# Cross-covariance attention and a multiplicative feed-forward: the start of batch one in another order

## The chip, the cores and the metric

The kernel runs on one core of one Trainium2 chip. The metric is the device time of one execution in microseconds (us). A core has five engines that run side by side: TensorE (PE, matmuls; PEld are its weight loads), VectorE (DVE), ScalarE (ACT), GpSimd (POOL) and SyncE (SP). Each works through its own list of instructions in order; an instruction waits for semaphores, and whatever stands behind it on its engine waits too. Transfers are issued by SP, ACT or POOL and carried out by DMA engines. A transfer that changes the type (here fp32 in memory to bf16 on chip) is issued by POOL in this kernel, plain stores and transposing transfers by SP.

## The reference

Four batches of 5824 rows with 256 columns pass through attention over the columns, then all 23,296 rows through the feed-forward:

```
qn = q / (norm of q's columns + 1e-6);  kn likewise
s  = kn^T @ qn / tau                      # 256 x 256 per batch
a  = softmax(s, last axis)
x  = v @ a                                # 5824 x 256 per batch
out = ((x @ w1) * (x @ w2)) @ w3 @ w_out  # 256 -> 1024 -> 1024 -> 256
```

tau is 1. All matrices come in fp32 and the output is fp32.

## The kernel before

**Two foldings of weights.** The kernel never computes x. It multiplies each batch's softmax matrix into w1 and w2 once (`fold`, `narrow`; the result is `Wf`), so that the products a = v @ (A w1) and b = v @ (A w2) come straight from v. Once for all batches it computes W = w3 @ w_out (`W_sb`, 1024 x 256), in eight units (`w_unit`), each of eight matmuls of 256 columns (L878). Each unit needs a part of w3 turned by a transposing transfer (`w3T_0` to `w3T_3`, two units each).

**Pieces and slots.** A batch of q, k or v is laid out with 45 rows to a partition and one short rest of 64 rows. It is loaded in six pieces: five of 8 rows per partition, and the last of 5 plus the rest (`LAST` is 5, the rest lies in the place behind). Loads round to bf16 on the way. Of v a piece must be turned, columns to partitions (`vT`): by TensorE in halves of four rows (`transpose_half_on_pe`, eight matmuls and a copy by VectorE) or by a transposing transfer of SP (`transpose_piece`).

The main loop goes over chunks of 512 rows (index `c`, two chunks to a piece) and, within a chunk, over eight blocks of 128 of the 1024 hidden columns (index `j`). One turn is a slot (`emit_ab`): two matmuls of 512 columns for `a`, two for `b`, a copy of `a` to bf16 by ScalarE (`as`, L662) and a multiply by VectorE (`abh`, L673). `a` and `b` use four PSUM banks in turn ("ab"); the folds, transpositions and W units mostly use three others ("out"). A slot's output matmuls come later (`pend`), in batch one only from slot 32 on, once W is there. From chunk 4 on a product scheme with seven instead of eight block products is used.

**The start of batch one.** There is nothing to compute on until q and k of batch one are on chip. TensorE follows their loads: `squares` (L259) accumulates q^T q, of which the diagonal gives the norms, and `products` (L271) accumulates q^T k into `G`. The squares of k are shared: for most of k ScalarE squares the rows and VectorE adds them up in `kacc` (L246, L247), for the end TensorE does it as for q. `busy` and `busy_long` are matmuls on constants that keep TensorE running while it waits for loads.

The functions of `soft_units(0)` then make the softmax matrix. Before the change: `k_early` folds `kacc` to 256 columns with a copy and an add (L282, L283), `k_first` takes the diagonal of k's squares and adds it (L287, L289), `k_row` sums over the partitions with a matmul against ones (L340, 256 columns in fp32) and turns the sum into 1/(root + 1e-6) in four ScalarE steps over 256 columns (L348: Ln, Exp with 0.5, Ln with 1e-6 added, Exp with -1). `q_first` reduces q's diagonal (L357), `scaled_first` multiplies `G` by k's factors (L379), makes q's factors and takes the exponentials (L384). `first_folds` and `second_quarter` make the first 512 columns of `Wf` in narrow steps, `soft0[8]` to `soft0[11]` the other 512 (L427).

The later batches have all the time of the batch before them and do the norms in another way: a reduce on VectorE which transposes blocks of 32 (L301), a small matmul against `fold4` (L309), the same four steps over 16 columns (L315), and a transposing copy that spreads the factors over the row (L322).

**What sets the order.** The order of instructions is that of the program's text. Within a batch an agenda (`at(t, cost, fn)`) holds steps with a due time against `clock`, which counts the time of TensorE's work as the program adds it up; at each slot `run_due` emits what is due. So a due time moves an instruction in every engine's list that it touches. POOL's list holds the loads, and between them small copies (`gate`, `hold`) whose only purpose is to make POOL wait: for a product of a slot, or for a transposing transfer. Eight loads of POOL are tracked at a time, so a load also waits for the landing of the eighth before it. SP's list holds the transposing transfers and the stores.

Before the change POOL issues, at the end of the start: q's last piece (its rest, then rows 0; 1 and 2; 3; 4), the first half of v's piece 0, w1 and w2 in column blocks 0 to 255, 256 to 511 and 512 to 1023, the second half of v's piece 0, v's pieces 1 and 2, w_out, w3. Slots run chunk by chunk, so chunk 0 needs all columns of w1 and w2 first, and chunk 1, from the second half of v's piece 0, comes at slot 8.

Of the kernel before, what the change touches and what calls it, by code (L numbers as in the profile page):

```python
# [10 lines left out]
ALU = mybir.AluOpType  # L11
# [3 lines left out]
P = 128  # L15
# [10 lines left out]
def kernel(  # L26
# [250 lines left out]
    def soft_units(n):  # L277
        st = {}

        def k_early():  # L280
            st["kk"] = work.tile([P, C], F32, tag="kk", name="kk", bufs=1)
            nc.vector.tensor_copy(st["kk"], kacc[0][:, 0, :])  # L282
            nc.vector.tensor_add(st["kk"], kacc[0][:, 1, :], st["kk"])  # L283

        def k_first():
            d = work.tile([P, CT, P], F32, tag="sq", name="dk", bufs=2)
            nc.vector.tensor_mul(d, S["k"], ident.unsqueeze(1).to_broadcast([P, CT, P]))  # L287
            d = st["ksq"] = d.rearrange("p c t -> p (c t)")
            nc.vector.tensor_add(d, d, st["kk"])  # L289

        def scaled_first():
            for ct in range(CT):
# [2 lines left out]
            exps(0)  # L295
            exps(1)

        def norms():

            red = work.tile([P, 16], F32, tag="red", name=f"red_{n}", bufs=1)  # L300
            nc.vector.tensor_reduce(  # L301
                out=red, in_=accs[n].rearrange("p w (b j) -> p (w b) j", j=32),
                axis=mybir.AxisListType.X, op=ALU.add, apply_transpose=True,
            )
            st["red"] = red

        def totals():
# [3 lines left out]
            )  # L311

        def norm_step(i):
            t = st["tot"][:, :16]
            nc.scalar.activation(  # L315
                out=t, in_=t, func=(AF.Ln, AF.Exp)[i % 2],
                scale=(1.0, 0.5, 1.0, -1.0)[i], bias=eps_t if i == 2 else 0.0,
            )

        def spread():  # L320
            st["kr"] = work.tile([P, C], F32, tag="kr", name=f"kr_{n}", bufs=1)
            nc.vector.transpose(  # L322
                st["kr"].rearrange("p (b j) -> p b j", j=32),
                st["tot"][:, 8:16].unsqueeze(2).to_broadcast([P, 8, 32]),
            )

        def pick():
# [9 lines left out]
        def k_row():  # L337

            m = psum.tile([P, 512], F32, name=f"row_{n}", **bank("ab"))
            nc.tensor.matmul(m[:, :C], lhsT=ones_pp, rhs=st["ksq"], start=True, stop=True)  # L340
            st["row"] = m[:, :C]
            st["kr"] = work.tile([P, C], F32, tag="kr", name=f"kr_{n}", bufs=1)
            for i in range(4):
                k_step(i)

        def k_step(i):
            kr = st["kr"]
            nc.scalar.activation(  # L348
                out=kr, in_=kr if i else st["row"], func=(AF.Ln, AF.Exp)[i % 2],
                scale=(1.0, 0.5, 1.0, -1.0)[i], bias=eps_t if i == 2 else 0.0,  # L350
            )

        def diagonal(src):
            d = work.tile([P, CT, P], F32, tag="sq", name=f"dq_{n}", bufs=2)
# [147 lines left out]
    def at(t, cost, fn):  # L502
        seq[0] += 1
        agenda.append((t, seq[0], cost, fn))
# [13 lines left out]
        return vTt[:, ct, :]  # L518

    last_ab = [None]  # L520
    halves = [None, None]
    slot = [0]
    due_sums = []
    following = []
# [125 lines left out]
    def emit_ab(b, c, j):  # L650
        n = chunk_cols(c)
        tiles = []
        for w in range(2):
            t = psum.tile([P, 512], F32, name=f"{'ab'[w]}_{b}_{c}_{j}", **bank("ab"))
            for ct in range(CT):
                nc.tensor.matmul(  # L656
                    t[:, :n], lhsT=Wf[b][:, ct, w, j * P : (j + 1) * P], rhs=rhs_of(b, c, ct),
                    start=(ct == 0), stop=(ct == CT - 1),
                )
            tiles.append(t)  # L660
        a_sb = work.tile([P, 512], BF16, tag="a_sb", name=f"as_{b}_{c}_{j}", bufs=4)
        nc.scalar.copy(a_sb[:, :n], tiles[0][:, :n])  # L662
        if c == NCH - 1:
            if b % 2 == 0 and j == 0:
                lefts[b // 2] = work.tile([P, FT, 2, P + LEFT], BF16, tag="left", name=f"left_{b}", bufs=1)
            both = lefts[b // 2][:, j, b % 2, :]
            nc.vector.tensor_mul(both, a_sb[:, :n], tiles[1][:, :n])
            ab = both[:, :P] if b % 2 == 0 else both[:, LEFT:]
        else:
            if j % 4 == 0:  # L670
                halves[j // 4] = in_pool.tile([P, 4, 512], BF16, tag="big", name=f"abh_{b}_{c}_{j}", bufs=BIG_BUFS)
            ab = halves[j // 4][:, j % 4, :]
            nc.vector.tensor_mul(ab, a_sb, tiles[1])  # L673
        last_ab[0] = ab
        slot[0] += 1
        if not seven(b, c):
            if b == B - 1 or c == NCH - 1:
                lag = LAG if b == B - 1 else FT + LAG_FAST
                pend.append((slot[0] + lag, 1, lambda only=None: emit_out(b, c, j, ab, only)))
            elif j == FT - 1:  # L680
                for i in range(FT):
                    fn = lambda i=i, ab2=tuple(halves): emit_half(b, c, i, ab2)
                    pend.append((slot[0] + 1 + LAG_FAST + i, 1, fn))
        elif j == FT - 1:
            sums, groups = seven_products(b, c, *halves)
            for i, fn in enumerate(sums):
                due_sums.append((slot[0] + 2 * i, fn))
            ready = slot[0] + 1 + (LAG_FAST if b < B - 1 else 0)
            for i, group in enumerate(groups):
                wait = 0 if b == B - 1 else i  # L690
                pend.append((ready + wait, 2, lambda group=group: [fn() for fn in group]))
        clock[0] += 4 * (n * MM_COL + MM_FIX)
# [94 lines left out]
    wout_sb = w3_wout[:, FT * F : FT * (F + D)].rearrange("p (l d) -> p l d", d=D)  # L787
    w3T = []

    def transpose_w3():  # L790

        for h in range(FT // 2):
            m = in_pool.tile([P, 2, FT, P], BF16, tag="big", name=f"w3T_{h}", bufs=BIG_BUFS)
            nc.sync.dma_start_transpose(m, w3_bf[:, 2 * h : 2 * h + 2, :])
            w3T.append(m)
# [39 lines left out]
    for pi in range(1, 4):  # L835
# [2 lines left out]
        products(pi, whole)  # L838
        if pi < 3:
            busy_long(pi)  # L840
    load_piece("q", 0, 5, (1, 3, 4))
    new_piece("v", 0, 0)
    load_part("v", 0, 0, 0, half)
    for f0, f1 in ((0, 256), (256, 512), (512, F)):
        nc.gpsimd.dma_start(out=w12[:, :, 0, f0:f1], in_=w1r[:, :, f0:f1])
        nc.gpsimd.dma_start(out=w12[:, :, 1, f0:f1], in_=w2r[:, :, f0:f1])
    load_part("v", 0, 0, half, PIECE)
    load_piece("v", 0, 1)
    load_piece("v", 0, 2)
    nc.gpsimd.dma_start(out=wout_sb, in_=moe_w_out.rearrange("(lh ll) c -> ll lh c", ll=P))  # L850
# [9 lines left out]
        squares("q", 4, sl)  # L860
        products(4, sl)
    soft0[1]()
    for sl in ([LAST, 0], [1, 2], [3]):
        squares("q", 5, sl)
        products(5, sl)
    squares("q", 5, [4], end=True)
    soft0[2]()
    products(5, [4], end=True)
    soft0[3]()
    soft0[6]()  # L870
    busy(2)
# [35 lines left out]
    def make_agenda(b):  # L907
# [3 lines left out]
        if b == 0:  # L911
            at(0.5, 0.87, soft0[5])
            for i in range(4):
                at((1.7, 2.6, 3.5, 3.9)[i], 0.43, soft0[8 + i])
            at(4.6, 0.5, lambda: transpose_half_on_pe(0, 0, 1, False))
            at(7.0, 0.5, lambda: transpose_half_on_pe(0, 1, 0, False))
            at(8.0, 0.5, lambda: transpose_half_on_pe(0, 1, 1, False))
            at(15.0, 0.0, transpose_w3)
            at(15.0, 0.0, lambda: transpose_piece(0, 2))
            for jt in range(FT):  # L920
                at(28.3 + 1.2 * jt, 0.87, lambda jt=jt: w_unit(jt))
            moves = [("qk", 1, 0, 29.0), ("qk", 1, 1, 29.2), ("v", 0, 3, 33), ("qk", 1, 2, 49), ("qk", 1, 3, 56)]
            moves += [("qk", 1, 4, 62), ("v", 0, 4, 68), ("qk", 1, 5, 79), ("v", 0, 5, 88)]
            moves += [("v", 1, 0, 99), ("v", 1, 1, 110), ("qk", 2, 0, 122)]
# [5 lines left out]

        for nm, m, pi, t in moves:
            if nm == "qk" and m == 1 and pi in (0, 2):
                at(t, 0.0, lambda pi=pi: hold(vTs[0][0][:1, (2 + pi // 2) * PIECE, 0, :1]))
            at(t, 0.0, gate)
            if nm == "qk":
                at(t, 0.0, lambda m=m, pi=pi: load_qk(m, pi))
            else:
                at(t, 0.0, lambda m=m, pi=pi: load_piece("v", m, pi))
                at(t + (2.5 if (m, pi) == (0, 4) else 4.0), 0.0, lambda m=m, pi=pi: transpose_piece(m, pi))
# [20 lines left out]

    for b in range(B):
        make_agenda(b)
        for c in range(NCH):
            for j in range(FT):
                run_due()
                while following:
                    following.pop(0)()
                scores_due(c * FT + j)
                emit_ab(b, c, j)
                lag = 0  # L970
                if b == B - 1 and c >= NCH - 2:
                    lag = LAG_END if c == NCH - 1 else LAG + (LAG_END - LAG) * (j + 1) // FT
                room = 2
                while slot[0] > W_SLOT and len(pend) > lag and pend[0][0] <= slot[0] and pend[0][1] <= room:
                    _, size, fn = pend.pop(0)
                    fn()
                    room -= size
                    run_due()
                while due_sums and due_sums[0][0] <= slot[0]:
                    due_sums.pop(0)[1]()  # L980
        run_due(1e9)

    n = len(pend)
# [37 lines left out]
```

## Time and profile before

| | |
|---|---|
| median of three executions | 556.06 us (555.81 to 557.0) |
| the profiled execution | 555.26 us |
| its span, first to last instruction | 553.5 us |
| TensorE busy in the span | 541.7 us (98%) |
| VectorE, ScalarE, GpSimd busy | 435.1, 376.8, 305.4 us |
| granted TensorE clock | 1.00 throughout |
| first matmul of `a` | 36.94 us after the span's start |
| k's last load of batch one lands | 28.97 us |
| moved by DMA | 77.61 MB, mean 140 GB/s |

The page's rows read: line of the program, engine, operation, output<-input with the shapes, count, then busy us in all, mean ns of one, and the idle time of the engine in front of them with what ended it. Rows of the order of instructions read: start and duration in us, engine, line, operation, and, in brackets, idle time before it. Rows of the chain of waits read: start, length in us, what it was. TensorE's matmuls are pipelined: the duration in a row is longer than the distance to the next row, and it is the distance that counts.

### The profile page before, as it was taken

What the parts mean: (1) busy time and instruction counts of PE and PEld (TensorE: products, weight loads), DVE (VectorE), ACT (ScalarE), POOL (GpSimd) and SP (SyncE); (2) the same over time, 40 slices, a digit from 0 to 9 for tenths busy, and PEclk for the clock granted to TensorE, in tenths of its full rate; (3) what the DMA queues carried; (4) which work ended last, traced back from release to release, by engine and by line L of the source; (5) the groups of instructions that cost most, each with busy time, mean ns of one, the idle gap of its engine ahead of it and who ended that gap; (6) DMA issues with size and microseconds to landing.
All of it is one profiled execution on the core that took longest, in us unless ns stands there. A gap on an engine that the chain in (4) does not pass through costs nothing.

```text
span 553.5 us, 12324 instructions
## 1 busy us (share of the span) xinstructions
PE 541.7 (98%) x4623; PEld 353.0 (64%) x4630; DVE 435.1 (79%) x787; ACT 376.8 (68%) x757; POOL 305.4 (55%) x259
## 2 busy tenths in 40 slices
PE   7799999999999999999999999999999999999997
PEld 4565577666666666666667566666666666666665
DVE  5558747899976787988876788888877688988984
ACT  5446647788866777777766777777766666566663
POOL 4260021778788678889887488898987400010000
PEclk9999999999999999999999999999999999999999
DMA  9999989985666878576554777775550245443102
GB/s 215 210 177 209 175 159 206 215 203 96 160 124 155 189 153 163 127 145 138 129 126 120 153 156 157 165 142 125 146 115 40 84 116 116 93 110 80 77 40 97
DMA packets 75260, 77.61 MB, mean 140 GB/s; under 512 B 54208, under 2 KB 59072, under 8 KB 75200
## 3 DMA queue, kind: packets, MB, share of 16 engines
q0 software_dynamic: 15904, 38.93, 40.2%
q1 hardware_dynamic: 58928, 37.17, 24.0%
q8 instruction: 36, 0.59, 0.4%
q10 hardware_dynamic: 368, 0.72, 0.4%
q14 instruction: 24, 0.20, 0.1%
HBM read 78.91 MB, written 23.86 MB: 186 GB/s over the span
## 4 chain that ended last, share of the span: by engine, by line
PE 93%; DMA 5%; DVE 0%; ACT 0%; issue 0%; POOL 0%; POOLq 0%
PE a L656 28%; PE b L656 28%; PE prodA L569 13%; PE prodC L569 6%; PE G L200 5%; PE prodB L569 3%; DMA k<-in_k_dram 3%; PE o L704 3%; PE fold L427 2%; DMA q<-in_q_dram 2%; PE o_out L735 2%; PE w L878 1%; PE G L271 0%; PE narrow L451 0%; POOL k L120 0%
## 5 line engine op out<-in xcount | busy, mean ns | idle before, releaser
L673 DVE TENSOR_TENSOR abh<-as,b 128x512 bf16<-128x512 bf16 x352 | 240.2, 684 | 82.8 <-ACT as L662 77.8
L662 ACT CAST as<-a 128x512 bf16<-128x512 f32 (+1 forms) x384 | 215.4, 562 | 93.7 <-PE a L656 61.4
L656 PE MATMUL a<-vT,Wf 128*128 128x512 bf16 x704 | 209.4, 379 | 0.1
L656 PE MATMUL b<-vT,Wf 128*128 128x512 bf16 x704 | 209.4, 379 | 0.0
L656 PEld LDWEIGHTS <-Wf 128*128 128x128 bf16 x1536 | 141.1, 98 | 100.6 <-issue 0.5
L569 PEld LDWEIGHTS <-S 128*128 128x128 bf16 x1248 | 82.6, 98 | 34.3 <-issue 0.2
L212 DVE TENSOR_TENSOR acc<-acc,sq 128x512 f32<-128x512 f32 x132 | 91.6, 694 | 3.0 <-ACT sq L197 1.9
L579 ACT COPY osb<-prodA 128x256 f32<-128x256 f32 x156 | 58.1, 372 | 42.0 <-PE prodA L569 41.4
L588 POOL TENSOR_TENSOR S<-abh,abh 128x1024 bf16<-128x1024 bf16 x29 | 61.7, 2126 | 31.7 <-DVE abh L673 16.6
L569 PEld LDWEIGHTS <-abh 128*128 128x128 bf16 x936 | 62.0, 98 | 25.7 <-issue 0.2
L591 POOL TENSOR_TENSOR S<-S,abh 128x1024 bf16<-128x1024 bf16 x29 | 61.7, 2127 | 1.9
L591 POOL TENSOR_TENSOR S<-abh,S 128x1024 bf16<-128x1024 bf16 x29 | 61.8, 2132 | 0.1
L591 POOL TENSOR_TENSOR S<-abh 128x1024 bf16<-128x1024 bf16 x29 | 61.8, 2130 | 0.1
L644 POOL COPY gate_t<-abh 1x1 bf16<-1x1 bf16 x39 | 7.2, 185 | 79.9 <-DVE abh L673 79.7
L569 PE MATMUL prodA<-comb_T,S 128*128 128x128 bf16 x624 | 47.6, 219 | 0.0
L200 PE MATMUL G<-k,q 128*128 128x256 bf16 x276 | 47.0, 273 | 0.0
L197 ACT ACTIVATE sq<-q 128x512 f32<-128x512 bf16 x69 | 43.8, 634 | 0.0
L197 ACT ACTIVATE sq<-k 128x512 f32<-128x512 bf16 x69 | 43.3, 628 | 0.0
L582 DVE TENSOR_TENSOR osb<-prodC,osb 128x256 f32<-128x256 f32 x78 | 32.6, 417 | 0.0
L648 POOL COPY gate_t<-vT 1x1 bf16<-1x1 bf16 x2 | 0.4, 176 | 53.1 <-DMA vT<-v 53.1
L200 PEld LDWEIGHTS <-q 128*128 128x128 bf16 x276 | 23.9, 98 | 3.6
L569 PE MATMUL prodB<-W_sb,abh 128*128 128x128 bf16 x312 | 23.8, 219 | 0.1
(137 smaller groups left out, 467.8 us busy)
## 6 DMA issues: line engine op xcount, KB each, us to landing
out_dram<-osb SPq DMA_DIRECT2D x44, 512.0 KB, 3.4
k<-in_k_dram POOLq DMA_DIRECT2D x19, 512.0 KB, 8.3
v<-in_v_dram POOLq DMA_DIRECT2D x19, 512.0 KB, 5.3
q<-in_q_dram POOLq DMA_DIRECT2D x18, 512.0 KB, 5.3
w_wout<-in_moe_w_dram POOLq DMA_DIRECT2D x1, 2048.0 KB, 22.4
k<-in_k_dram POOLq DMA_DIRECT2D x4, 320.0 KB, 7.0
v<-in_v_dram POOLq DMA_DIRECT2D x4, 320.0 KB, 5.4
q<-in_q_dram POOLq DMA_DIRECT2D x3, 320.0 KB, 5.0
```

Of the source, the lines that this page charges most:

```text
L197: nc.scalar.activation(out=sqs[0][:, :, part, :], in_=src[:, o : o + 2, :], func=AF.Square)
L200: nc.tensor.matmul(G[:, ct, :], lhsT=qt[:, i, ct * P : (ct + 1) * P], rhs=kt[:, i, :], start=(pr == 0 and part == 0 and ct == 0), stop=(pr ...
L212: nc.vector.tensor_add(accs[n], accs[n], sqs[0][:, part - 2])
L569: nc.tensor.matmul(st[nm][:, i, :], lhsT=a[:, j, i * P : (i + 1) * P], rhs=w[j], start=(first and j == 0 and i == 0), stop=(j == 3), skip_ ...
L579: nc.scalar.copy(quarter(r, d), st["A"])
L582: nc.vector.tensor_add(quarter(r, d), st[nm], quarter(r, d))
L588: adder.tensor_add(x, a21, a22)
L591: adder.tensor_sub(x, u, w)
L656: nc.tensor.matmul(t[:, :n], lhsT=Wf[b][:, ct, w, j * P : (j + 1) * P], rhs=rhs_of(b, c, ct), start=(ct == 0), stop=(ct == CT - 1),)
L662: nc.scalar.copy(a_sb[:, :n], tiles[0][:, :n])
L673: nc.vector.tensor_mul(ab, a_sb, tiles[1])
L704: nc.tensor.matmul(t[:, k, :], lhsT=ab2[j // 4][:, j % 4, (2 * h + k) * P : (2 * h + k + 1) * P], rhs=W_sb[:, j, :], start=(j == 0 and k = ...
```

## The change

It has six parts, all of them in batch one.

1. The norms of k are made as in the later batches: `k_early` and `k_first` reduce with transposition (to eight columns), `k_row` multiplies by `fold4`, takes the four steps over eight columns in PSUM, and spreads.
2. q's last piece comes in two transfers besides its rest (rows 0 to 2; 3 and 4) instead of four, and the last squares of q are those of rows 3 and 4 together, ahead of the products of both.
3. The second half of v's piece 0 is loaded ahead of the columns 512 to 1023 of w1 and w2, instead of after them.
4. The first 16 slots go by halves: chunk 0 with j = 0 to 3, chunk 1 with j = 0 to 3, chunk 0 with j = 4 to 7, chunk 1 with j = 4 to 7. The two tiles of a chunk's products are allotted together at j = 0. The due times of v's transpositions and of the last four folds move with this.
5. Of the transposing transfers, v's piece 2 goes ahead of the last part of w3; the two W units that need this part are due later, behind slot 32.
6. GpSimd's hold before the loads of batch 2's first q and k waits for the last part of w3 instead of v's piece 2.

```diff
         def k_early():
-            st["kk"] = work.tile([P, C], F32, tag="kk", name="kk", bufs=1)
-            nc.vector.tensor_copy(st["kk"], kacc[0][:, 0, :])
-            nc.vector.tensor_add(st["kk"], kacc[0][:, 1, :], st["kk"])
+            red = work.tile([P, 16], F32, tag="red", name="red_acc", bufs=1)
+            partition_sums(red, kacc[0].rearrange("p w (b j) -> p (w b) j", j=32))
+            st["kk"] = work.tile([P, 8], F32, tag="kk", name="kk", bufs=1)
+            nc.vector.tensor_add(st["kk"], red[:, :8], red[:, 8:])
 
         def k_first():
             d = work.tile([P, CT, P], F32, tag="sq", name="dk", bufs=2)
             nc.vector.tensor_mul(d, S["k"], ident.unsqueeze(1).to_broadcast([P, CT, P]))
-            d = st["ksq"] = d.rearrange("p c t -> p (c t)")
-            nc.vector.tensor_add(d, d, st["kk"])
+            red = work.tile([P, 16], F32, tag="red", name="red_end", bufs=1)
+            partition_sums(red[:, :8], d.rearrange("p c (b j) -> p (c b) j", j=32))
+            st["ksq"] = work.tile([P, 8], F32, tag="ksum", name="ksum", bufs=1)
+            nc.vector.tensor_add(st["ksq"], red[:, :8], st["kk"])
...
+        def partition_sums(dst, src):
+
+            nc.vector.tensor_reduce(out=dst, in_=src, axis=mybir.AxisListType.X, op=ALU.add, apply_transpose=True)
+
+        def root_step(t, i):
+
+            nc.scalar.activation(
+                out=t, in_=t, func=(AF.Ln, AF.Exp)[i % 2],
+                scale=(1.0, 0.5, 1.0, -1.0)[i], bias=eps_t if i == 2 else 0.0,
+            )
...
         def k_row():
 
             m = psum.tile([P, 512], F32, name=f"row_{n}", **bank("ab"))
-            nc.tensor.matmul(m[:, :C], lhsT=ones_pp, rhs=st["ksq"], start=True, stop=True)
-            st["row"] = m[:, :C]
-            st["kr"] = work.tile([P, C], F32, tag="kr", name=f"kr_{n}", bufs=1)
+            t = m[:, :8]
+            nc.tensor.matmul(t, lhsT=fold4.rearrange("p g j -> p (g j)"), rhs=st["ksq"], start=True, stop=True)
             for i in range(4):
-                k_step(i)
...
+                root_step(t, i)
+            spread(t)
...
-            if j % 4 == 0:
-                halves[j // 4] = in_pool.tile([P, 4, 512], BF16, tag="big", name=f"abh_{b}_{c}_{j}", bufs=BIG_BUFS)
-            ab = halves[j // 4][:, j % 4, :]
+            if j == 0:
+                halves[c] = [
+                    in_pool.tile([P, 4, 512], BF16, tag="big", name=f"abh_{b}_{c}_{h}", bufs=BIG_BUFS) for h in range(2)
+                ]
+            ab = halves[c][j // 4][:, j % 4, :]
...
-    load_piece("q", 0, 5, (1, 3, 4))
+    load_piece("q", 0, 5, (3,))
     new_piece("v", 0, 0)
     load_part("v", 0, 0, 0, half)
     for f0, f1 in ((0, 256), (256, 512), (512, F)):
         nc.gpsimd.dma_start(out=w12[:, :, 0, f0:f1], in_=w1r[:, :, f0:f1])
         nc.gpsimd.dma_start(out=w12[:, :, 1, f0:f1], in_=w2r[:, :, f0:f1])
-    load_part("v", 0, 0, half, PIECE)
+        if f0 == 256:
+            load_part("v", 0, 0, half, PIECE)
...
-    for sl in ([LAST, 0], [1, 2], [3]):
+    for sl in ([LAST, 0], [1, 2]):
         squares("q", 5, sl)
         products(5, sl)
-    squares("q", 5, [4], end=True)
+    squares("q", 5, [3, 4], end=True)
     soft0[2]()
-    products(5, [4], end=True)
+    products(5, [3, 4], end=True)
...
-                at((1.7, 2.6, 3.5, 3.9)[i], 0.43, soft0[8 + i])
-            at(4.6, 0.5, lambda: transpose_half_on_pe(0, 0, 1, False))
-            at(7.0, 0.5, lambda: transpose_half_on_pe(0, 1, 0, False))
-            at(8.0, 0.5, lambda: transpose_half_on_pe(0, 1, 1, False))
-            at(15.0, 0.0, transpose_w3)
+                at((5.3, 6.2, 7.1, 8.0)[i], 0.43, soft0[8 + i])
+            at(2.5, 0.5, lambda: transpose_half_on_pe(0, 0, 1, False))
+            at(11, 0.5, lambda: transpose_half_on_pe(0, 1, 0, False))
+            at(14, 0.5, lambda: transpose_half_on_pe(0, 1, 1, False))
+            at(15.0, 0.0, lambda: transpose_w3(range(FT // 2 - 1)))
             at(15.0, 0.0, lambda: transpose_piece(0, 2))
+            at(15.0, 0.0, lambda: transpose_w3([FT // 2 - 1]))
             for jt in range(FT):
-                at(28.3 + 1.2 * jt, 0.87, lambda jt=jt: w_unit(jt))
+                t = 28.3 + 1.2 * jt if jt < FT - 2 else 37.0 + 1.3 * (jt - FT + 2)
+                at(t, 0.87, lambda jt=jt: w_unit(jt))
...
-                at(t, 0.0, lambda pi=pi: hold(vTs[0][0][:1, (2 + pi // 2) * PIECE, 0, :1]))
+                at(t, 0.0, lambda pi=pi: hold(w3T[-1][:1, 0, 0, :1] if pi == 0 else vTs[0][0][:1, 3 * PIECE, 0, :1]))
...
-        for c in range(NCH):
-            for j in range(FT):
+        order = [(c, j) for c in range(NCH) for j in range(FT)]
+        if b == 0:
+            order[: 2 * FT] = [(c, h * 4 + j) for h in range(2) for c in range(2) for j in range(4)]
+        for s, (c, j) in enumerate(order):
```

More of the change, by code (lines that the diff above doesn't have):

```diff
@@ L296, in scaled_first @@
             exps(1)
+        def partition_sums(dst, src):
[5 more added lines that the diff above has]
+            )
         def norms():
             red = work.tile([P, 16], F32, tag="red", name=f"red_{n}", bufs=1)
[L301 to L304, printed above, removed]
+            partition_sums(red, accs[n].rearrange("p w (b j) -> p (w b) j", j=32))
             st["red"] = red
@@ L313, in norm_step, with spread @@
         def norm_step(i):
[L314 to L320, printed above, removed]
+            root_step(st["tot"][:, :16], i)
+        def spread(src=None):
+            src = st["tot"][:, 8:16] if src is None else src
             st["kr"] = work.tile([P, C], F32, tag="kr", name=f"kr_{n}", bufs=1)
@@ L323, in spread @@
                 st["kr"].rearrange("p (b j) -> p b j", j=32),
-                st["tot"][:, 8:16].unsqueeze(2).to_broadcast([P, 8, 32]),
+                src.unsqueeze(2).to_broadcast([P, 8, 32]),
             )
@@ L339, in k_row @@
             m = psum.tile([P, 512], F32, name=f"row_{n}", **bank("ab"))
-            nc.tensor.matmul(m[:, :C], lhsT=ones_pp, rhs=st["ksq"], start=True, stop=True)
-            st["row"] = m[:, :C]
-            st["kr"] = work.tile([P, C], F32, tag="kr", name=f"kr_{n}", bufs=1)
+            t = m[:, :8]
+            nc.tensor.matmul(t, lhsT=fold4.rearrange("p g j -> p (g j)"), rhs=st["ksq"], start=True, stop=True)
             for i in range(4):
-                k_step(i)
[L346 to L351, printed above, removed]
+                root_step(t, i)
+            spread(t)
         def diagonal(src):
@@ L520 @@
     last_ab = [None]
-    halves = [None, None]
+    halves = {}
     slot = [0]
@@ L681, in emit_ab @@
                 for i in range(FT):
-                    fn = lambda i=i, ab2=tuple(halves): emit_half(b, c, i, ab2)
+                    fn = lambda i=i, ab2=tuple(halves[c]): emit_half(b, c, i, ab2)
                     pend.append((slot[0] + 1 + LAG_FAST + i, 1, fn))
         elif j == FT - 1:
-            sums, groups = seven_products(b, c, *halves)
+            sums, groups = seven_products(b, c, *halves[c])
             for i, fn in enumerate(sums):
@@ L788, with transpose_w3 @@
     w3T = []
-    def transpose_w3():
-        for h in range(FT // 2):
+    def transpose_w3(parts):
+        for h in parts:
             m = in_pool.tile([P, 2, FT, P], BF16, tag="big", name=f"w3T_{h}", bufs=BIG_BUFS)
@@ L962 @@
         make_agenda(b)
-        for c in range(NCH):
-            for j in range(FT):
-                run_due()
[L966 to L980, printed above, removed]
+        order = [(c, j) for c in range(NCH) for j in range(FT)]
+        if b == 0:
+            order[: 2 * FT] = [(c, h * 4 + j) for h in range(2) for c in range(2) for j in range(4)]
+        for s, (c, j) in enumerate(order):
+            run_due()
+            while following:
+                following.pop(0)()
+            scores_due(s)
+            emit_ab(b, c, j)
+            lag = 0
+            if b == B - 1 and c >= NCH - 2:
+                lag = LAG_END if c == NCH - 1 else LAG + (LAG_END - LAG) * (j + 1) // FT
+            room = 2
+            while slot[0] > W_SLOT and len(pend) > lag and pend[0][0] <= slot[0] and pend[0][1] <= room:
+                _, size, fn = pend.pop(0)
+                fn()
+                room -= size
+                run_due()
+            while due_sums and due_sums[0][0] <= slot[0]:
+                due_sums.pop(0)[1]()
         run_due(1e9)
```

## The prediction

> **What bounds the kernel now.** I read the page first, then TensorE's order of instructions and the chain of waits over the first 110 us, then the landings of single transfers.
>
> The page: TensorE is busy 541.7 of 553.5 us.
>
> ```profile
> span 553.5 us, 12324 instructions
> PE 541.7 (98%) x4623; PEld 353.0 (64%) x4630; DVE 435.1 (79%) x787; ACT 376.8 (68%) x757; POOL 305.4 (55%) x259
> PE 93%; DMA 5%; DVE 0%; ACT 0%; issue 0%; POOL 0%; POOLq 0%
> ```
>
> The 11.8 us that are left lie at two ends. The table of stages gives TensorE 8.12, 7.05, 8.28 and 9.20 of the first four tens of us, 9.95 of the fifth and then 10.00 of each ten up to 160 us; 540 to 554 has 9.42 of 14. A busy matrix row could still hide slow matmuls, so I looked at the spacing: from the first `a` (36.94) on, each pair of 512-column matmuls starts 0.43 to 0.44 us after the one before it, through slots, folds, transposes and W, at a granted clock of 1.00. There is no hole left. A change in this place can therefore gain only what it takes from the time before the first `a`, and it loses every us that it makes TensorE wait behind it. The chain of waits there, by start and length:
>
> ```profile
> 13.27 15.70 DMA k<-in_k_dram
> ...
> 29.01 0.84 PE sqk L259 x12
> ...
> 31.20 0.43 PE row L340 x2
> ...
> 33.28 0.12 PE sqq L259 x2
> ...
> 33.43 0.24 DVE dq L357
> ...
> 33.94 0.67 DVE s L379 x2
> ...
> 34.94 0.52 ACT e L384
> ...
> 36.94 0.60 PE a L656 x2
> ```
>
> To 28.97 us the loads of q and k rule; then TensorE works without a hole to the last squares of q (33.40), and from there a string of short steps runs to the first `a`, 3.5 us later. The string hangs on the last squares of q (`dq`), not on the last products.
>
> **The change, part by part.**
>
> *k's norms.* Three prices, of the row matmul, of its counterpart in the later batches (`tot`, L309), and of the later batches' reduce, step and spread:
>
> ```profile
> 31.03 0.60 PE L340 MATMUL row<-dk,ones_pp 128*128 128x256 f32 x2
> ...
> 154.83 0.35 PE L309 MATMUL tot<-red,fold 128*128 128x16 f32 x2
> 155.03 0.59 PE L656 MATMUL a<-vT,Wf 128*128 128x512 bf16 x2
> ...
> L301 DVE TRANSPOSE_TENSOR_REDUCE red<-acc 128x16 f32<-128x512 f32 x3 | 2.1, 709 | 0.0
> ...
> L315 ACT ACTIVATE tot<-tot 128x16 f32<-128x16 f32 x9 | 1.7, 185 | 0.0
> ...
> L322 DVE STREAM_TRANSPOSE kr<-tot 128x256 f32<-128x256 f32 x3 | 1.3, 443 | 0.0
> ```
>
> TensorE's next instruction starts 0.44 us after the row matmul (31.47), and 0.20 us after `tot`: 0.24 us gained on the path. VectorE before it: the early part, copy and add (0.42 + 0.42), becomes reduce and add (0.71 + 0.17), ending near 29.2 where `dk` starts at 29.89, so covered by the wait for k's squares; without that cover it would cost 0.04. The end part is multiply, reduce of 256 columns, add of 8. No row has that reduce: from below 0.42, what any 256-column fp32 operation here takes (L287, 425 ns), from above the 0.71 of 512 columns. I take 0.44. Steps on VectorE start 0.04 after the one before ends, so `ksum` is there at 29.89 + 0.46 + 0.48 + 0.17 = 31.00, just before TensorE asks (31.03). With 0.71 TensorE would wait 0.25 us, with q's last squares queued behind. ScalarE's four steps fall from 1.8 us (31.67 to 33.49) to about 0.92 (three of 0.185, one of 0.257, gaps of 0.04), from about 31.44 to 32.36. The new spread (0.44) then ends at 32.84. It stands ahead of `dq` on VectorE, which is ready for it only at 32.99 (below): 0.15 us to spare, and any lateness above that falls on the chain.
>
> *q's end.* Squares of slots 3 and 4 now come together ahead of both products. Before, products of slot 3 (two matmuls, 0.22) lay in front of the last squares. So the last squares end 0.24 + 0.22 = 0.46 earlier less rounding; I count 31.25 (end of the new row) + two double slots at 0.66 + 0.22 for four squares, with VectorE starting 0.31 after the last pair starts as before: 32.99 against 33.43, 0.44 gained. G is complete near 33.40, before `s` wants it (33.50), so the 0.44 passes on to `e` and `a`.
>
> *q's last piece in two transfers, not four.* The single transfers, KB landed and us from issue to landing (issues at 23.95, 26.28, then 27.51 and 28.03 as one row's neighbours, and v's half at 29.25):
>
> ```profile
> q<-in_q_dram POOLq DMA_DIRECT2D x1, 64.0 KB, 6.9
> q<-in_q_dram POOLq DMA_DIRECT2D x1, 128.0 KB, 5.2
> q<-in_q_dram POOLq DMA_DIRECT2D x1, 64.0 KB, 4.3
> q<-in_q_dram POOLq DMA_DIRECT2D x2, 64.0 KB, 4.2
> v<-in_v_dram POOLq DMA_DIRECT2D x1, 256.0 KB, 4.2
> ```
>
> They land at 30.85, 31.48, 31.8, 32.2, 33.45, in order, 0.3 to 0.4 us per 64 KB, so the queue never ran dry. The first new part (slots 0 to 2) is whole when the second old one was, 31.40 to 31.48; the faster TensorE asks for slot 0 at 31.36. I charge 0.08. The second part (32.0 to 32.2) is asked for at 32.7: covered by 0.5. The Trainium skill (DMA: Bandwidth & Descriptors, Bandwidth) has a 64 KB transfer take 0.95 us and wants transfers batched to a MiB. By that, two transfers fewer would bring the loads some 1.1 us forward, and my 0.08 would be 0; the rows show 0.33 to 0.42 for each in a full queue, so I keep the charge. Even by the rule the gain stays 0.44, as TensorE is the limit there. GpSimd saves two issues of 0.53 us, which nobody waits for.
>
> *Weights behind v, two chunks by halves.* Before, w1's last columns were issued at 32.74 and landed 6.4 later (39.14), asked for at 39.55; w2's landed near 40.4, asked for at 41.28; v's second half 34.13 + 7.5 = 41.6, asked for at 43.01. No stall there, so nothing to gain; the order moves margins. With the change v's second half follows the four 128 KB weights (last landing 36.5) by the 1.2 us that a half takes: 37.7. It is asked for after slot 1, at 36.6 + 0.87 + 0.87 + 0.87 = 39.2: 1.5 to spare. The last columns then land at 40.4 and 41.6, asked for at 41.9 and 44.5. v's second piece keeps all bytes ahead of it (44.1) and is asked for near 48.
>
> Slots 0 to 15 do the same instructions in another order. I went through banks with ScalarE at 0.59 and VectorE at 0.69 per step. Two folds now stand in one slot (before the eighth), ScalarE evicts both ahead of `as` of that slot, so its multiply ends about 11.36 after the first `a`, while the matmul that takes over its bank is due at 11.28. I charge 0.08 (0 to 0.15).
>
> *w3, v's piece 2, W's last columns.* The four turns of w3 and that of v are issued by SP 2.4 us apart from 59.06; v's landed at 73.69 and slot 32 asked at 74.63. Now v goes fourth: about 71.3, asked for at 73.5; w3's last about 73.5, asked for by the moved W unit at about 74.7. Both covered, by 2.2 and 1.2 (before 0.9). Moved units are the same 16 matmuls. On GpSimd the first hold now waits for w3's last turn, 73.5 instead of 73.7; q and k of batch 1 queue behind it and are asked for at 84. The tiles of the products are only allotted sooner, and the steps after slot 33 keep their order.
>
> *Sum*: -0.24 - 0.20 + 0.08 + 0.08 = -0.28 us. The profiled execution took 555.26 us, its span 553.5 and 1.76 around it; the sum makes 553.2 and 554.98. The median shown, 556.06, is 0.8 above the profiled execution; I subtract there too: 555.78, say 555.75.
>
> **The rivals.**
>
> *A. A wait that this execution doesn't show goes away; faster.* The other executions are 0.55 to 1.7 us longer than the profiled one. If part of that is TensorE waiting for w1's last columns (0.4 to spare) or for v's piece 2 (0.9), the new order removes it: 0.28 plus some 0.8, 554.95. Against it: lateness of the first 29 us of loads moves everything alike, and then the change saves none of it.
>
> *B. v's second half lands late; slower.* The transposition stands in TensorE's queue right after slot 1, everything behind it. It lands at 37.7 only if the queue keeps its order against the weights issued right after. If they share the engines, it lands with them, near 41, as the three did before (39.1 to 41.6): TensorE stands 1.8 us, net 1.5 slower, 557.6. It decides from a landing at 39.5 (no gain) and from 40.6 (over 0.2%). Against it: the landings in order above.
>
> *C. The norms chain is as slow as before.* If the reduce takes 0.71, `row` stalls 0.25, spread ends at 33.1, and with the two charges at their upper ends nothing is left: 556.0 to 556.1.
>
> *D. DVE or ScalarE becomes the bound in slots 4 to 15*: their work per slot stays under the 0.87 of TensorE; 0.3 lost at most, no gain, 556.1. Counted with C.
>
> **How the numbers follow.** Likeliest case 0.56 (its own range 555.3 to 556.3, as three executions scatter by 1.2), A 0.18, B 0.13, C and D 0.13. 0.2% is 1.1 us, about what a measurement can tell from no change. Faster by more: A and the tail of the likeliest, 0.23. Slower by more: B with a little scatter, 0.14. Within: 0.63. The range reaches down past A's 554.95, to 554.7, and up to 557.1, which takes in the upper ends of all charges with the scatter, but not B's full price.
>
> **What would show it.** The row matmul followed by q's squares 0.2 us later; `dq` at about 33.07 and the first `a` at about 36.6 where it was 36.94; no wait of TensorE for v's second half; slot 32 straight after the sixth W unit; the last matmul 0.3 earlier. Wrong if the transposition after slot 1 is preceded by idle TensorE on a landing of v, if `dq` starts on the end of the spread, or if the first `a` is earlier but the span is not.

## The result and the profile after

Median 555.12 us (16 executions, 554.99 to 555.37) against 556.83 us before (16 executions, 555.25 to 558.12). The ratio is 0.9972 with a 95% interval of 0.9964 to 0.9981: the changed kernel is 1.0 to 2.0 us faster. It is also much steadier: its executions lie within 0.4 us of each other, those before within 2.9.

The two profiled executions cannot show that: their spans are equal. The page after, span, engines, and the chain's shares by engine:

```profile
span 553.5 us, 12330 instructions
PE 542.1 (98%) x4630; PEld 352.9 (64%) x4630; DVE 435.5 (79%) x789; ACT 375.8 (68%) x757; POOL 304.8 (55%) x257
PE 93%; DMA 5%; DVE 0%; ACT 0%; POOL 0%; issue 0%; POOLq 0%
```

The chain of waits after (start, length, what), the steps that were shown of before:

```profile
13.27 16.00 DMA k<-in_k_dram
...
29.32 0.84 PE sqk L259 x12
...
31.48 0.27 PE row L349 x2
31.75 0.29 PE sqq L259 x4
...
33.13 0.24 PE sqq L259 x4
...
33.90 0.68 DVE s L380 x2
...
34.90 0.52 ACT e L385
...
36.89 0.60 PE a L657 x2
```

Here k landed at 29.27, in the profile of before at 28.97. From that landing to the first `a` it took 7.97 us before and takes 7.62 now, 0.35 less; the later landing hides it. So the short chain at the start is worth about what was worked out. Over 1 us of the gain is still missing, and it has to lie in executions that are not like the one profiled before: that one ran in 555.26 us, next to the shortest of sixteen.

VectorE's order in the changed kernel, for the new steps on it (start, duration, line, operation):

```profile
30.66 0.45 DVE L303 TRANSPOSE_TENSOR_REDUCE red_end<-dk 128x8 f32<-128x256 f32 x1
31.14 0.17 DVE L292 TENSOR_TENSOR ksum<-red_end,kk 128x8 f32<-128x8 f32 x1
32.64 0.45 DVE L330 STREAM_TRANSPOSE kr<-row 128x256 f32<-128x256 f32 x1 [1.33 <-ACT row L307]
33.39 0.29 DVE L358 CUSTOM_DVE_ANT_0 dq<-sqq,ident 128x128 f32<-128x128 f32 x1 [0.31 <-PE sqq L259]
```

The reduce of 256 columns takes 0.45 us (0.44 was assumed), and VectorE stands idle for 0.31 us between the spread and `dq`, so the spread is off the chain.

### The profile page after: what moved, and what is told of

It is laid out like the page before. It is cut to its first block, busy times and chain, and to the rows that moved or that the text cites. A ratio compares the mean times of both kernels' runs of the same rounds, so it can differ in the third digit from the quotient of the medians.

```text
span 553.5 us, 12330 instructions
## 1 busy us (share of the span) xinstructions
PE 542.1 (98%) x4630; PEld 352.9 (64%) x4630; DVE 435.5 (79%) x789; ACT 375.8 (68%) x757; POOL 304.8 (55%) x257
## 4 chain that ended last, share of the span: by engine, by line
PE 93%; DMA 5%; DVE 0%; ACT 0%; POOL 0%; issue 0%; POOLq 0%
PE a L657 28%; PE b L657 28%; PE prodA L570 13%; PE prodC L570 6%; PE G L200 5%; PE prodB L570 3%; DMA k<-in_k_dram 3%; PE o L707 3%; PE fold L428 2%; DMA q<-in_q_dram 2%; PE o_out L738 2%; PE w L882 1%; PE G L271 0%; PE narrow L452 0%; PE sqq L259 0%
## 5 line engine op out<-in xcount | busy, mean ns | idle before, releaser
L570 PE MATMUL prodC<-comb_T,S 128*128 128x128 bf16 x312 | 23.8, 219 | 0.0
```

Of the source, the lines that this page charges most:

```text
L570: nc.tensor.matmul(st[nm][:, i, :], lhsT=a[:, j, i * P : (i + 1) * P], rhs=w[j], start=(first and j == 0 and i == 0), stop=(j == 3), skip_ ...
```

## The experiments

There were eleven runs of 9 to 12 executions each, two of them of the kernels before and after once more. They ran on three chips, each run beside 29 or more executions of the kernel before on the same chip; the medians of before there were 556.57, 556.73 and 556.53 us. Ratios are to these.

**The kernel before, again**, without an edit, for a profile of a longer execution.

> The kernel before, once more, to see one of its longer executions in a profile. Its 16 executions reach from 555.25 to 558.12 us; the profiled one (555.26) is among the shortest. All theories expect a median near 556.8. Theory W (TensorE waits in some executions for the last columns of w1, which were there only 0.4 us before they were asked for): a longer execution has idle TensorE before the fold into columns 512 and up, near 39.5 us, of 1 to 2 us. Theory V (it waits for v's piece 2 at slot 32, 0.9 us to spare): idle TensorE near 74.6 us. Theory L (the loads of the first 29 us scatter): the first a comes later by the whole excess, and nothing is idle after it.

556.52 us (555.44 to 557.61); the profiled execution took 556.63, its span 554.8. The first `a` came at 36.92, where it was in the short execution. What differs is slot 32. Its `a` in TensorE's order in the short execution of before, then here:

```profile
74.63 0.59 PE L656 MATMUL a<-vT,Wf 128*128 128x512 bf16 x2
```

```profile
75.98 0.60 PE L656 MATMUL a<-vT,Wf 128*128 128x512 bf16 x2 [1.12 <-DMA vT<-v]
```

SP's order here (start, duration), then the turn of v in the chain of waits (start, length):

```profile
59.99 9.65 SPq L794 DMA_TRANSPOSE w3T<-w_wout  x4
69.70 2.57 SPq L166 DMA_TRANSPOSE vT<-v  x1
```

```profile
69.70 6.24 DMA vT<-v
```

SP's order in the short execution of before:

```profile
59.06 9.58 SPq L794 DMA_TRANSPOSE w3T<-w_wout  x4
68.69 2.50 SPq L166 DMA_TRANSPOSE vT<-v  x1
```

TensorE waits until v's piece 2 is turned: 1.12 us in the row, 1.28 by the distance to the rows before it (it was due at 74.70), and that is the whole difference between the two spans (554.8 and 553.5). The turns of w3 started 0.93 later, because w3 itself landed later, and the turn of v took 6.2 us to land where it took 5.0. The 0.9 us that v's piece 2 had to spare in the short execution is used up. Theory V had the right place. Theories W and L fall for this execution: the view of waits names no other wait of TensorE after the first `a`, and the first `a` is not late. Nothing above 556.8 us was profiled, while single executions reach 558.1; what those lose is open.

Why did the turn itself take longer? The single packets of the DMA queues show it. A turn ends with 16 pairs of packets of 4 bytes. Here fifteen pairs were over at 73.80, but the last one came only at 74.84, at the very end of a packet of 16 KB of the queue "instruction", which ran from 73.92 to 74.85:

```profile
DMA packets 4, 0.02 MB, mean 8 GB/s; under 512 B 3, under 2 KB 3, under 8 KB 3
q8 instruction: 1, 0.02, 2.8%
q1 hardware_dynamic: 3, 0.00, 0.2%
```

(That is the stretch from 73.9 to 76 us: this packet and three tiny ones.) In the short execution the packet started at 73.02, just when the last pair ended. In five profiles, this one among them, the last pair of a turn comes only as the packet ends, and these are the five turns that took 6.2 to 6.7 us; in all other profiles the turn in that place took 4.6 to 5.0. So a late w3 costs more than its delay: it moves the end of the turn to where this packet runs. Without the 1.04 us by which the last pair came late, some 0.2 of the 1.28 would be left (an estimate from these times). No run takes the packet away, so this last link is read from the traces and is not tested.

**Parts 3 and 4 undone** in the changed kernel.

```diff
-        if f0 == 256:
-            load_part("v", 0, 0, half, PIECE)
+    load_part("v", 0, 0, half, PIECE)
...
-            order[: 2 * FT] = [(c, h * 4 + j) for h in range(2) for c in range(2) for j in range(4)]
+            pass
```

> The changed kernel with its parts 3 and 4 undone: weights ahead of v's second half, chunks one after the other, old due times of folds and transpositions; norms, q's end and the order of w3 as changed. Theory W: the scatter of the kernel before is back, at least half of its executions over 556, median 556.0 to 556.8, since the folds ask 0.3 us earlier than before. Theory V or L: as tight as the changed kernel, 555.0 to 555.4.

555.03 us (554.86 to 555.38), ratio to before 0.9976 [0.9967, 0.9986]. Nothing is lost without the new order of slots and loads.

**Parts 5 and 6 undone** in the changed kernel.

```diff
-            at(15.0, 0.0, lambda: transpose_w3(range(FT // 2 - 1)))
+            at(15.0, 0.0, lambda: transpose_w3(range(FT // 2)))
             at(15.0, 0.0, lambda: transpose_piece(0, 2))
-            at(15.0, 0.0, lambda: transpose_w3([FT // 2 - 1]))
...
```

The lines left out give the two W units and the hold their old places.

> The changed kernel with its parts 5 and 6 undone: all four turns of w3 ahead of v's piece 2, W units and hold as before. Theory V: the scatter is back, median 556.0 to 556.8. Theory W or L: as tight as the changed kernel, 555.0 to 555.4, since slot 32 keeps about 0.6 us to spare.

555.06 us (554.91 to 555.29), 0.9975 [0.9966, 0.9984]. This contradicts my expectation for theory V: with v's piece 2 behind all of w3 again, slot 32 still does not wait. Its profile says why: the first turn of w3 is issued at 57.54, 1.5 us sooner than in the short execution before and 2.5 sooner than in the longer one. The waiting place is slot 32, but something ahead of w3 has changed.

**Parts 3 and 4 alone**, on the kernel before.

> The kernel before with parts 3 and 4 alone: v's second half ahead of the last columns, the first 16 slots by halves. Theory W: tight, about 0.3 above the changed kernel, 555.3 to 555.7. Theory V: scatter as before, median near 556.8. Theory L: scatter as before, as the first 29 us and the norms are those of before.

556.51 us (555.64 to 557.17), 0.9999 [0.9990, 1.0007]. No gain. In its profile w3's first turn is issued at 60.11, slot 32 waits 1.00 us for v, and the narrow folds ahead of the first `a` wait for the first columns of w2 as well:

```profile
PE a L661 <- DMA vT<-v: 1.0, 1, 1.0
...
PE narrow L456 <- DMA w<-in_moe_w_dram: 0.2, 1, 0.2
```

What is left are parts 1 and 2. The profile of the changed kernel suggests which of the two it is. GpSimd's order before and after, from v's first half on (start, duration, and the wait before it):

```profile
29.25 0.53 POOL L120 DMA_DIRECT2D v<-in_v_dram  x1 [0.69 <-DMA k<-in_k_dram]
29.94 0.70 POOL L845 DMA_DIRECT2D w<-in_moe_w_dram  x1 [0.16 <-issue]
30.63 0.72 POOL L846 DMA_DIRECT2D w<-in_moe_w_dram  x1
```

```profile
27.82 0.53 POOL L120 DMA_DIRECT2D v<-in_v_dram  x1 [0.71 <-DMA q<-in_q_dram]
28.34 0.71 POOL L848 DMA_DIRECT2D w<-in_moe_w_dram  x1
29.55 0.71 POOL L849 DMA_DIRECT2D w<-in_moe_w_dram  x1 [0.51 <-DMA k<-in_k_dram]
```

Each load waits until the eighth before it has landed: before, v's half waits for k's last piece, issued at 13.27, eight loads ahead. With two loads fewer, it waits for an earlier load, of q. It is issued 1.4 us sooner, the four loads of weights behind it 1.1 to 1.6 us sooner, w_out and w3 still 0.6. The table of stages shows what the transfers made of it; the stage 31 to 40 us before and after (the last number is GB/s):

```profile
31.00:40.00 9.00, 8.20 (x78) 5.81 (x78) 4.72 (x15) 5.74 (x13) 6.57 (x10) 1.00 1.13 164
```

```profile
31.00:40.00 9.00, 8.48 (x88) 6.20 (x86) 5.46 (x18) 4.74 (x13) 5.49 (x8) 1.00 1.25 206
```

164 GB/s against 206, where both have 204 and 207 in the stage 20 to 31 us. The difference over 9 us is 0.38 MB, at 206 GB/s some 1.8 us of transfers (an estimate); w3's turns start 1.3 us (short execution) to 2.2 us (longer one) sooner. The next runs test that reading.

**Two transfers alone.** The kernel before with one edit.

```diff
-    load_piece("q", 0, 5, (1, 3, 4))
+    load_piece("q", 0, 5, (3,))
```

> The kernel before with one edit: q's last piece in two transfers besides its rest instead of four. Theory Q (two loads fewer let GpSimd issue v's half and the weights over 1 us sooner, each load being issued on the landing of the eighth before it; the transfer queue no longer runs low from 31 to 40 us, w3 is there 1.5 to 2.5 us sooner, and TensorE's wait at slot 32 for v's piece 2 goes): tight, 555.3 to 555.6, w3's first turn issued near 57.6, no wait at slot 32. Theory N (the norms bring it): scatter as before, median near 556.6.

555.40 us (555.20 to 555.58), 0.9976 [0.9967, 0.9984]: tight, 1.33 us under the 556.73 of before beside it. In its profile SP issues w3's first turn at 57.59, and TensorE has no wait on any transfer after the first `a`. The first `a` itself is not earlier (37.09, 7.98 after k's landing).

**Norms and squares without it.** Part 1 and the new order of the last squares on the kernel before, four transfers.

```diff
...
-    for sl in ([LAST, 0], [1, 2], [3]):
+    for sl in ([LAST, 0], [1, 2]):
...
-    squares("q", 5, [4], end=True)
+    squares("q", 5, [3, 4], end=True)
```

The lines left out at the top are part 1 as in the change.

> The kernel before with k's norms by transposing sums and the order of q's last squares, but with the four transfers, the old load order, slots and order of w3. Theory Q: scatter as before, median 556.3 to 556.8; the first a comes 0.3 sooner, but slot 32 still waits for v's piece 2, so nothing of the 0.3 is left in the longer executions. Theory N: tight, 555.0 to 555.4.

556.34 us (555.38 to 558.22), 0.9996 [0.9985, 1.0007]. The first `a` comes 7.82 us after k's landing, 0.21 of it a wait for w2's first columns; slot 32 then waits longer. TensorE's waits from 60 us on:

```profile
PE a L657 <- DMA vT<-v: 1.2, 1, 1.2
```

What the start gains is given back at slot 32, because v's piece 2 comes when the transfers bring it. The turn took 6.3 us here, again with the packet of 16 KB ahead of its last pair.

**The order of w3 alone.** Parts 5 and 6 on the kernel before.

> The kernel before with parts 5 and 6 alone: v's piece 2 turned ahead of the last part of w3, the two W units and the hold moved. Theory Q: v's piece 2 lands about 2.4 us sooner, which covers the 1.1 us that slot 32 waited, whenever w3 comes: tight, 555.3 to 555.6, although w3's first turn is issued at 59 to 60. If the excess of the longer executions has another place, the scatter stays, median near 556.6.

555.84 us (555.39 to 556.84), 0.9991 [0.9982, 1.0000]. Between both expectations: 0.9 under the before beside it by the medians, 0.5 by the ratio, and the interval reaches no change. Its profile is of an execution of 555.70: w3's first turn is issued at 59.46 and slot 32 does not wait, but the chain of waits goes through the turn that is now last, that of w3:

```profile
69.18 6.27 DMA w3T<-w_wout
75.45 0.04 issue
75.50 1.05 PE w L885 x8
```

It took 6.3 us, again with the packet of 16 KB ahead of its last pair. The moved W unit starts 0.71 us after the products ahead of it instead of 0.43, so the wait has gone to another place and is 0.28 us long there.

**Two transfers and two tiny ones.** The kernel of the two transfers with two loads of 16 bytes behind them, which nothing reads.

```diff
     load_piece("q", 0, 5, (3,))
+    for i in range(2):
+        dummy = work.tile([1, 4], F32, tag=f"dummy{i}", name=f"dummy{i}", bufs=1)
+        nc.gpsimd.dma_start(out=dummy, in_=q[0, i : i + 1, :4])
```

> As the run with two transfers for q's last piece, with two loads of 16 bytes issued right behind them, so that as many loads as before stand ahead of v's half. Theory Q by count: v's half is issued near 29.2 again, on k's landing, w3's first turn near 59 to 60, scatter, median near 556.6. Theory Q by size (longer rows per transfer make the queue faster): as the run without the tiny loads, 555.3 to 555.6.

556.41 us (555.59 to 557.33), 0.9995 [0.9987, 1.0004]. 32 bytes undo the whole gain. GpSimd's order in it:

```profile
27.54 1.03 POOL L844 DMA_DIRECT2D dummy<-in_q_dram  x2 [0.69 <-DMA q<-in_q_dram]
29.25 0.56 POOL L120 DMA_DIRECT2D v<-in_v_dram  x1 [0.68 <-DMA k<-in_k_dram]
```

v's half is back at 29.25, waiting for k; the stage 31 to 40 us is down to 157 GB/s (204 in the run with the two transfers alone), w3's first turn at 60.24. So it is the number of loads that counts, not their bytes. The rows show two ways in which it does: the two issues alone take GpSimd 1.03 us, and then v's half waits 0.68 us more for k. No run parts the two.

What then makes the executions long differs. In its profile (556.12 us) w3 is the latest of all, and yet slot 32 does not wait: its turn took 4.8 us, its last pair was over before the packet of 16 KB. TensorE lost time nearer to the start instead, 0.34 us of it here (and about 0.5 us in two more places up to 45 us):

```profile
36.16 0.33 PE L451 MATMUL narrow<-w,e 128*128 128x128 bf16 x3 [0.34 <-DMA w<-in_moe_w_dram]
```

**Four transfers in the changed kernel.** The reverse edit.

```diff
-    load_piece("q", 0, 5, (3,))
+    load_piece("q", 0, 5, (1, 3, 4))
```

> The changed kernel with one edit undone: q's last piece again in four transfers besides its rest. Theory Q: GpSimd issues v's half near 29.2 again, on k's landing, w3's first turn is issued at 59 to 60, scatter comes back in part: v's piece 2 stays ahead of the last part of w3, so slot 32 is covered, but the first weights and the moved W unit are short, 555.4 to 556.0. If the other five parts were enough: 555.0 to 555.3, tight.

555.89 us (555.41 to 556.51), 0.9992 [0.9982, 1.0002]. All other parts are there, but by the medians about half of the gain is gone (by the ratios two thirds), and the scatter is back. v's piece 2 is in time at slot 32, but w3's first turn is issued at 60.12 and the wait has moved one place on, to the W unit that needs w3's last part:

```profile
PE w L882 <- DMA w3T<-w_wout: 1.0, 1, 1.0
```

It is the place of the order of w3 alone, and that turn too took 6.3 us, with the packet ahead of its last pair.

**Parts 1 and 2 alone**, on the kernel before, beside **the changed kernel again**.

> The kernel before with parts 1 and 2 alone (norms, q's end in two transfers and its squares in one go); load order, slots and order of w3 as before. Theory Q: all that the change brings, 554.9 to 555.2, tight; 0.3 to 0.4 under the run with two transfers alone, which is the worth of the shorter chain. If halves or the order of w3 bring anything on top: 555.3 or more.

> The changed kernel once more, beside the other two on the same chip: 555.0 to 555.3, tight.

555.02 us (554.88 to 555.11), 0.9975 [0.9966, 0.9984], and 555.10 us (555.02 to 555.43), 0.9976 [0.9967, 0.9984]. Parts 1 and 2 bring everything. In their profile it is 7.60 us from k's landing to the first `a`, against 7.98 with the two transfers alone, and the span is 553.2 us against 553.6. The medians differ by as much, 0.38, but are from two chips, and the ratios (0.9975 and 0.9976) cannot part the two kernels. Nor can they tell whether parts 1 and 2 are faster than the full change. One known loss of the full change is small: in the profile of the full change the `b` of the slot behind two folds follows its `a` after 0.56 us instead of 0.43.

| kernel | median, us | v's half issued | w3's first turn issued | first a |
|---|---|---|---|---|
| before, profiled 555.26 | 556.83 | 29.25 | 59.06 | 36.94 |
| before again, profiled 556.63 | 556.52 | 29.17 | 59.99 | 36.92 |
| 3 and 4 alone | 556.51 | 29.19 | 60.11 | 37.19 |
| two transfers and two tiny | 556.41 | 29.25 | 60.24 | 37.34 |
| norms and squares | 556.34 | 29.31 | 60.11 | 36.85 |
| changed, four transfers | 555.89 | 29.35 | 60.12 | 36.64 |
| 5 and 6 alone | 555.84 | 29.19 | 59.46 | 36.91 |
| two transfers alone | 555.40 | 27.70 | 57.59 | 37.09 |
| changed | 555.12 | 27.82 | 57.77 | 36.89 |
| changed, 5 and 6 undone | 555.06 | 27.61 | 57.54 | 36.67 |
| changed, 3 and 4 undone | 555.03 | 27.62 | 57.53 | 36.66 |
| 1 and 2 alone | 555.02 | 27.66 | 58.21 | 36.71 |

The third column sorts the kernels by itself: those that issue v's half before 28 us are at 555.4 or below and tight, the others are at 555.8 or above and scatter. (The medians were not all taken on the same chip, so differences of 0.2 us between rows mean nothing; the last three columns are of one execution each.)

## Why the prediction was right and wrong

The time, 555.12, lies in the range and 0.6 below the 555.75 predicted, but that closeness is in part luck. The prediction started from 556.06, the median of three executions, where sixteen gave 556.83; and it took off 0.28 us where 1.71 came off. The first makes the forecast 0.8 us too low, the second 1.4 too high, and what is left of the two is the 0.6. The likeliest case was a gain too small to measure; what came, 0.28% by the ratio, is in size that of rival A, priced at 554.95, which had 0.18. Rival A had the right place too, v's piece 2 at slot 32, but not what took the wait away. By its steps:

- *What bounds it*: right for the profiled execution, wrong as a statement about the kernel. "There is no hole left" behind the first `a` holds in one of the shortest executions; the longer one has a hole of 1.3 us at slot 32. The prediction had the sign before it, the profiled execution 0.8 under the median of three, and the 0.9 us to spare at this place, and put both into a rival instead of into the sum.
- *k's norms and q's end*: right. From k's landing to the first `a` 0.36 was forecast (0.44 less 0.08), 0.35 came in the profiles, 0.38 between the runs with and without. With all four transfers kept (the reverse edit) it was 7.57: 0.40 of the 0.44 came, and the two transfers cost 0.03 to 0.06 of the 0.08 charged.
- *q's last piece in two transfers*: this is the step that failed. It said that the transfers land in order every 0.3 to 0.4 us, "so the queue never ran dry", and that GpSimd's two issues are saved where "nobody waits for" them. In fact v's half and all weights stand behind these two issues, and with them v's half waits for a later landing than without; the queue ran low, 164 instead of 206 GB/s between 31 and 40 us. The rows from which the prediction read a full queue show landings in order, and these come from a low queue too: the loads issued from 27.5 to 32 us landed 4.1 to 4.7 us after their issue, where those of the changed kernel from 27.8 to 32 us took 5.4 to 6.0 at the higher rate, and most loads before 21 us took 12 to 19. The step should have brought 1.3 us (556.73 to 555.40) of the 1.7. The rule of the Trainium skill that was weighed there (DMA: Bandwidth & Descriptors, Bandwidth) points the right way, but the run with two tiny loads shows that the time of small transfers is not the mechanism here. That its 1.1 us is near the 1.1 to 1.6 us by which the loads moved is then chance.
- *Weights behind v, chunks by halves*: worth nothing was right: neither alone nor taken out does it move the time beyond what the runs can tell. v's second half was issued at 31.66 and landed 6.0 us later (37.7, as forecast), so rival B has no place.
- *Two folds in one slot*: 0.08 charged, 0.13 seen.
- *w3 and v's piece 2*: covered, as forecast. Rival A expected that this order takes the wait away. Alone it does so for slot 32, but in its profile the wait goes to the moved W unit, and its gain of 0.5 to 0.9 us is not clear of no change; in the changed kernel it has nothing to do, since w3 comes 1.3 to 2.2 us sooner anyway.
- *Rival C*: fell. The reduce takes 0.45, the spread has 0.31 us to spare.

Three things stay open. Why w3 lands, and its turn is issued, at 59.0 in one execution of the kernel before and at 60.0 in another was not settled; in no profile with two transfers in place of four, and no tiny ones, was its turn issued later than 58.2. What part of the loss is GpSimd's time for two issues and what part the wait for a landing was not parted. And that the packet of 16 KB holds up the end of a turn is read from its times alone.

## What to carry to other kernels

In this kernel a load cost its place among the eight that are tracked, and its time of issue, whether it moved 64 KB or 16 bytes, so a few small loads delayed all transfers behind them. Look at what a load's *issue* waits for, and read from the rate of each stage whether the queue is full: landings in order don't show it. Where single executions scatter by more than the effect that is forecast, the one profile is a draw: list every wait that it avoided by less than the scatter, and put those into the sum. A gain ahead of a place that waits for transfers is given back there; first look for what feeds the transfers. And where one transfer takes longer than its equals, look at what else ran on the queues just then.

## What the runs showed that was not expected

Two loads of 16 bytes, read by nothing, lengthened the median by 1.0 us (555.40 to 556.41). With them the transfers between 31 and 40 us fell from 204 to 157 GB/s; the changed kernel fell from 206 to 159 with its two loads split into four. And in five profiles a turn of 512 KB, which otherwise took 4.6 to 5.0 us, took 6.2 to 6.7, with one packet of 16 KB of the queue "instruction" ahead of its last few bytes.
